# A projection slot between the value product and the score pair, and half-row groups 19 slots apart

## The chip, the core and the metric

The kernel runs on one core of a Trainium2 chip. Its engines work side by side, each through its own list of instructions: PE multiplies matrices (its weight loads are shown as PEld), DVE and ACT work element by element and both read PE's results out of PSUM, POOL masks, and SP issues the DMA transfers. The metric is the device time of one execution in microseconds (us); the time of a kernel is the median of its runs.

## The reference

One layer mixes sliding-window attention and a gated linear unit, weighted per token by a gate. There are 2048 tokens of 512 features, 32 heads of 16 features, a window of 256 tokens, and 1376 hidden features. All of it is float32.

```
x = A_x
g = sigmoid((x * gate_w).sum(-1, keepdims=True))
q, k, v = heads of x @ wqkv
scores = q k^T * 16 ** -0.5, masked to 0 <= i - j < 256
a = (softmax(scores) @ v) @ wo
b = (sigmoid(x @ w_gate) * (x @ w_up)) @ w_down
return g * a + (1 - g) * b
```

## The kernel before

**Precision.** A float32 operand is split into a rounded high part and a remainder, and a product is the sum of three matmuls (high by high, high by low, low by high). Features come in four blocks of 128 (`ND`), so one result tile of 128 by 512 takes 12 matmuls: such a set of 12 is called a group here.

**Stages.** The attention runs over `u` from 0 to 139 (`N`), in units of a group of four heads and a block of 128 tokens; there are 128 such units (`NU`). At `u`, `s_part(u, hh)` computes the scores of one head with queries on the partitions, and DVE takes their row maximum (`junk`, L307). `st_part(u - 9, hh)` computes the scores of an earlier unit transposed, with the maximum built into the operands, and ACT turns them into exponentials (`pt`, L352). POOL masks them. At every second `u`, ahead of the first head, `pv_part` multiplies the exponentials of the two units at `u - 12` and `u - 11` with V (L380): four heads side by side, each in a strip of 32 result columns, summed up in one bank `pv`. ACT then copies out half of `pv` (`o_take`, L396), and DVE clears it.

`s` and `st` of one iteration are a pair: each contracts over 64 rows, one in the upper and one in the lower half of the array, so that they run together. This is called a score pair.

**Slots.** Between the score pairs PE works off 111 groups: the projections of later heads (`pj`) and the gate and up products (`gu`). Each is cut into an upper and a lower half of its 128 contracted rows. The generator `turns()` counts slots `t`. In slot `t` it issues the upper-half matmul number `t`, and the lower-half matmul number `t - SHIFT`, which belongs to an earlier group; the two run together. A group's upper halves thus take slots 12i to 12i + 11 and its lower halves slots 12i + 18 to 12i + 29. A group holds one of three PSUM banks called `misc` from its first slot until ACT has copied it out. The generator yields after every third slot (`GAP`). The loop calls it once per head, not after the last head of an odd `u`: seven chunks of three slots in two `u`. From `u` = 128 on there are no more `s`, and it is called twice after every second head.

**Order.** The order on PE, ACT, DVE and SP is the order in which the program issues; the scheduler does not change it. Three lists put work off: `acts` (for ACT) and `behind` (for DVE) give up one entry at each head, and `later` holds stores, which SP issues at the start of the next `u`. When a group has its last slot, `turns()` puts its `post` (the copy out of PSUM) and its `after` (the next weights' rounding, where there is one) at the head of `acts`. They are issued in the next iteration, behind that one's score pair and exponential.

**The end.** A gate or up result goes out to scratch memory, and a last stage loads it again, multiplies with `w_down` (`pd`) and adds the attention part (`pa`). Three groups (`HOLD`) are kept back, with all 128 rows at once, to fill PE around the last value product.

Of the kernel before, what the change touches and what calls it, by code (L numbers as in the profile page):

```python
# [36 lines left out]
PVLAG = LAG + 2  # L37
# [1 line left out]
QB = 32  # L39
HOLD = 3  # L40
GAP = 3
SHIFT = 18
WD_LATE = {1: 8, 2: 9, 5: 10}
AHEAD = 5

# [2 lines left out]
def gated_mix_kernel(  # L48
# [48 lines left out]
    NU = NG * NB  # L97
# [20 lines left out]
    with ExitStack() as actx:  # L118
# [142 lines left out]
        def stack_build(t):  # L261
            sh, sl = (v.bitcast(F32) for v in stg.pop(t))
            rt = ring[t % RING].bitcast(F32)
            st = rt.rearrange("(a r) j f -> r a j f", r=4)
            dmas = [fill_rows(t % RING, 0, 0)]
            for low in range(2):
                for j in range(4):
                    for r in range(3):
                        if low == (r == (1 if j < 2 else 2)):
                            dmas.append((st[r + 1, :, j], (sl if low else sh)[32 * j:32 * j + 32]))  # L270
            return dmas

        def run_dmas(dmas):
            for dst, src in dmas:
                nc.sync.dma_start(dst, src)
# [92 lines left out]
        acts = []  # L368
        obs = {}

        def pv_part(u):
            g, j = divmod(u, NB)
            p = pts.pop(u)
            last = min(NB, j + 3)
            q = j
            while q < last:
                e = min(last, (q // 4 + 1) * 4)
                for hh in range(HG):
                    h = g * HG + hh
                    mm(  # L380
                        pv[32 * hh:32 * hh + 32, (q % 4) * P:(q % 4 + e - q) * P],
                        V[:, j, h * VW:h * VW + 32],
                        p[:, hh, (q - j) * P:(e - j) * P],
                        start=False, stop=True, skip_group_check=True,
                        tile_position=(0, 32 * hh),
                    )
                q = e
            if j % 2 == 1:
                acts.insert(0, lambda: o_take(g * NC + j // 4, j // 2 % 2))

        def o_take(s, half):
            g, c = divmod(s, NC)
            if half == 0:
                obs[s] = cpool.tile([P, CH], F32, tag="ob", name=f"ob{s}", bufs=2)
            cols = slice(2 * P * half, 2 * P * half + 2 * P)
            nc.scalar.copy(obs[s][:, cols], pv[:, cols])  # L396
            behind.insert(0, lambda: nc.vector.memset(pv[:, cols], 0.0))
            if half == 0:
                return
            ob = obs.pop(s)  # L400
            for hh in range(HG):
                h = g * HG + hh
                later.append((oT_d[h * DH:(h + 1) * DH, c * CH:(c + 1) * CH], ob[32 * hh:32 * hh + DH]))
            later.append((sum_d[c, g * HG:(g + 1) * HG], ob.rearrange("(h r) f -> r h f", r=32)[DH]))
# [38 lines left out]
        def load_gu(f, w):  # L443
            raw_gu[f, w] = cpool.tile([P, D], F32, tag="draw", name=f"guraw{f}_{w}", bufs=2)
            src = wgu[f, w] if FCH[f] == P else wgu_tail[w, :, :, 0:width(f, w)]
            nc.sync.dma_start(gu_half(raw_gu[f, w], width(f, w)), src)
# [72 lines left out]
        def turns():  # L519
            k3 = 3 * ND  # L520
            groups = []
            for t in range(n_rest * k3 + SHIFT):
                if t and t % GAP == 0:
                    yield
                if t % k3 == 0 and len(groups) < n_rest:
                    groups.append((work or rest).pop(0))
                for half, v in enumerate((t, t - SHIFT)):
                    if 0 <= v < n_rest * k3:
                        groups[v // k3][0](v % k3, half)
                if t >= SHIFT and (t - SHIFT) % k3 == k3 - 1:  # L530
                    _, after, post = groups[(t - SHIFT) // k3]
                    acts.insert(0, lambda after=after, post=post: (post(), after()))

        def flush(acts):
            while acts:
# [25 lines left out]
        def flat(v, c):  # L561
            return v[c].rearrange("h (q t) -> (h q) t", t=P)
# [5 lines left out]
        def sums_invert(c):  # L568
            t = sm.pop(c)
            nc.vector.reciprocal(t, t)  # L570
            return flat(rec_d, c), t

        def hold_group(step, _, post):
            for k in range(3 * ND):
                step(k)
            post()
# [7 lines left out]
        WD = NU - 5  # L584
        done = 0
        slots = turns()
        sdma = []

        for u in range(N):
            if u == LAG:  # L590
                vctx.close()
                ppool = actx.enter_context(tc.tile_pool(name="ppool", bufs=1))
            if u == 4:
                load_gu(0, 0)
                load_gu(0, 1)
            if u % 8 == 1 and u > 8 and u // 8 + 1 < NP:
                sdma = stack_build(u // 8 + 1)
            if u % 16 == 8 and u // 16 + 2 < NG:
                raw_q = load_wqk(u // 16 + 2)
            if u % 4 == 0 and 0 < u <= NU:  # L600
                max_store(u // 4 - 1)
            run_dmas(later)
            later.clear()
            run_dmas(sdma[:SD])
            del sdma[:SD]
            if u % 4 == 1 and 1 < u <= NU + 1:
                max_load(u // 4 - 1)
            if WD <= u < WD + 16 and (u - WD) % 2 == 0:
                load_d((u - WD) // 2)
            s4 = {1: 4, 5: 5, 9: 6, U_LAST: NSTEP - 2, U_LAST + 1: NSTEP - 1}.get(u)  # L610
            if u % 4 == 3 and u > LAG and (u + 2) // 4 + 4 < NSTEP - 2:
                s4 = (u + 2) // 4 + 4
            if s4 is not None:
                if u < LAG:
                    (work if u == 1 else first).append((3 * ND, lambda k, s4=s4: proj_mm(s4, k), lambda s4=s4: proj_post(s4)))
                else:
                    work.append(proj_group(s4))
            if u == NU + PVLAG - 1:
                hold_group(*rest.pop(0))
            for hh in range(HG):  # L620
                if hh == 0 and u % 2 == 0:
                    for w in (u - PVLAG - 1, u - PVLAG):
                        if 0 <= w < NU:
                            pv_part(w)
                if u < NU:
                    s_part(u, hh)
                if 0 <= u - LAG < NU:
                    st_part(u - LAG, hh ^ 1 if u < NU else hh)
                if u < LAG:
                    flush(behind)  # L630
                else:
                    if behind:
                        behind.pop(0)()
                    if acts:
                        acts.pop(0)()
                if u >= LAG and (hh < HG - 1 or u % 2 == 0 if u < NU else hh % 2 == 1):
                    next(slots, None)
                    if u >= NU:
                        next(slots, None)
            if u < LAG - 1:  # L640
                done += run_first(n_first * (u + 1) // LAG - done)
            elif u < LAG:
                run_first(n_first - done - 3 * ND)
                split_gu(0, 0)
                split_gu(0, 1)
                flush(acts)
                flush(behind)
                run_first(3 * ND)
                done = 0
            if u % 4 == 3 and u < NU:  # L650
                max_split(u // 4)
            if u // 16 + 2 < NG:
                if u % 16 == 13:
                    acts.append(lambda g=u // 16 + 2, r=raw_q: (
                        split_wqk(g, r, 0), behind.append(lambda: split_wqk(g, r, 1))))
            if 0 <= u - LAG < NU:
                mask_p(u - LAG)
            if WD + 2 <= u < WD + 10 and (u - WD) % 2 == 0:
                acts.append(lambda f=(u - WD) // 2 - 1: split_d(f, True))
            if SUMS <= u and (u - SUMS) % 4 == 0:  # L660
                sums_load((u - SUMS) // 4)
            if SUMS + 2 <= u and (u - SUMS) % 4 == 2:
                behind.append(lambda c=(u - SUMS) // 4: later.append(sums_invert(c)))
            if u >= HLOAD and (u - HLOAD) % 2 == 0:
                h_load((u - HLOAD) // 2)
            if u >= N - 2:
                flush(acts)
                flush(behind)
                h_skew(u - N - 1)
# [160 lines left out]
```

## Time and profile before

| | us |
|---|---|
| median of 3 runs | 756.0 |
| lowest and highest run | 755.45, 757.91 |
| the profiled execution | 755.79 |
| its span, first to last instruction | 754.1 |
| PE busy in the span | 745.9 |
| DVE busy | 483.7 |
| ACT busy | 436.2 |
| POOL busy | 171.9 |

In the lines of the profile, L233 is line 233 of the kernel. In the order in time, the columns are the start in us, the duration in us, the engine, the line, the operation, result and operands, the rows and columns of the array that a matmul or a weight load uses (64*128 is half the rows), and shapes; square brackets give the engine's idle time before it and what ended that. "x4" marks a run of equal instructions told as one. A matmul's start is recorded and its end is modelled. A weight load stands as PEld, ahead of its matmul. In the row by stage, the columns are the stretch and its length, then busy time and number of instructions of PE, PEld, DVE, ACT and POOL, PE's granted clock, and the DMA engines' busy share and rate. In a row that groups instructions, "mean ns" is the duration of one.

### The profile page before, as it was taken

The page shows a single profiled execution, that of the slowest core. Times are in us where ns is not written, and L with a number is a line of the kernel's source. Part 1 is how long each engine was busy: PE and PEld are TensorE (multiplying, and loading weights), DVE is VectorE, ACT ScalarE, POOL GpSimd, SP SyncE. Part 2 cuts the span into 40 slices and gives each one's busy share as a digit, 9 for nine tenths or more (in the row PEclk, how much of TensorE's full clock was granted, in tenths as well). Part 3 has the DMA queues.
Part 4 walks back from the last instruction along what each step waited for, and adds up shares of the span by engine and source line. Part 5 has one row for each costly group of instructions (what it writes and reads, how often), then busy time and mean ns, then how long its engine had stood idle before and what let it go on. Part 6 is the DMA issues. An engine that isn't in the chain of part 4 may idle for free.

```text
span 754.1 us, 17424 instructions
## 1 busy us (share of the span) xinstructions
PE 745.9 (99%) x6180; PEld 582.1 (77%) x6180; DVE 483.7 (64%) x1459; ACT 436.2 (58%) x930; POOL 171.9 (23%) x256
## 2 busy tenths in 40 slices
PE   8999999999999999999999999999999999999997
PEld 6877777787777877788787877778776778888886
DVE  5356767776776766776677676677522885749381
ACT  5412666666676667666666666656665562616241
POOL 7000233233233233323323322332321000000000
PEclk9999999999999999999999999999999999999999
DMA  8340434426444453444543525433455967557351
GB/s 305 95 113 19 108 100 120 124 76 172 120 105 125 118 143 111 115 112 123 139 126 85 149 68 162 141 108 118 128 179 157 270 214 224 178 190 226 122 154 56
DMA packets 69959, 103.58 MB, mean 137 GB/s; under 512 B 19314, under 2 KB 29042, under 8 KB 69872
## 3 DMA queue, kind: packets, MB, share of 16 engines
q1 hardware_dynamic: 69872, 102.48, 46.5%
q8 instruction: 48, 0.79, 0.4%
q14 instruction: 39, 0.32, 0.2%
HBM read 45.26 MB, written 32.00 MB: 102 GB/s over the span
## 4 chain that ended last, share of the span: by engine, by line
PE 95%; DMA 2%; DVE 1%; SPq 1%; issue 0%; ACT 0%; DVEq 0%; ACTq 0%
PE gu L233 34%; PE pj L233 12%; PE pv L380 11%; PE s L301 8%; PE st L347 5%; PE pd L70 4%; PE pd L72 4%; PE pd L71 4%; PE vps L70 2%; PE vps L72 2%; PE vps L71 2%; PE pa L70 2%; PE pa L72 2%; PE pa L71 2%; DMA woraw<-in_wo_dram 1%; DMA V<-in_xT_dram 1%
## 5 line engine op out<-in xcount | busy, mean ns | idle before, releaser
L307 DVE CUSTOM_DVE_ANT_0 junk<-s,mask 128x384 f32<-128x384 f32 (+2 forms) x512 | 272.1, 531 | 142.4 <-PE s L301 80.2
L233 PE MATMUL gu<-xh,w 64*128 64x512 f32 (+2 forms) x1384 | 344.4, 392 | 0.0
L352 ACT ACTIVATE pt<-st 128x384 f32<-128x384 f32 (+2 forms) x512 | 242.1, 474 | 170.4 <-PE st L347 69.9
L233 PE MATMUL gu<-xl,w 64*128 64x512 f32 (+3 forms) x692 | 227.4, 392 | 0.0
L233 PEld LDWEIGHTS gu<-xh,w 64*128 64x128 f32 (+2 forms) x1384 | 190.1, 183 | 19.5 <-issue 0.4
L357 POOL TENSOR_SCALAR_AFFINE_SELECT pt<-pt 128x512 f32<-128x512 f32 x128 | 88.1, 689 | 384.3 <-ACT pt L352 384.3
L347 PE MATMUL st<-ring 64*128 64x384 f32 (+2 forms) x536 | 169.7, 332 | 0.0
L301 PE MATMUL s<-ring 64*128 64x384 f32 (+2 forms) x536 | 165.7, 332 | 0.0
L301 PEld LDWEIGHTS s<-ring 64*128 64x128 f32 x536 | 94.4, 184 | 39.0 <-DVE nm L317 12.5
L233 PEld LDWEIGHTS gu<-xl,w 64*128 64x128 f32 (+3 forms) x692 | 107.9, 183 | 5.4
L347 PEld LDWEIGHTS st<-ring 64*128 64x128 f32 x536 | 97.1, 184 | 12.1 <-issue 2.7
L233 PE MATMUL pj<-xh,wqh 64*128 64x512 f32 (+1 forms) x232 | 91.5, 399 | 1.1 <-ACT xh L66 1.1
L380 PE MATMUL pv<-pt,V 128*32 128x384 f32 (+2 forms) x1408 | 91.0, 388 | 0.0
L233 PE MATMUL pj<-xl,wqh 64*128 64x512 f32 (+1 forms) x232 | 90.9, 397 | 0.0
L362 POOL TENSOR_SCALAR_AFFINE_SELECT pt<-pt 128x512 f32<-128x512 f32 x112 | 74.2, 663 | 0.0
L233 PE MATMUL pj<-xh,wql 64*128 64x512 f32 (+1 forms) x232 | 70.9, 392 | 0.0
L70 PE MATMUL pd<-ring,hb 128*128 128x512 f32 (+1 forms) x176 | 69.7, 396 | 1.1 <-ACT hb L66 1.1
L72 PE MATMUL pd<-ring,hb 128*128 128x512 f32 (+1 forms) x176 | 69.2, 393 | 0.5 <-DVE hb L67 0.4
L71 PE MATMUL pd<-ring,hb 128*128 128x512 f32 (+1 forms) x176 | 68.6, 390 | 0.4 <-DVE ring L111 0.4
L380 PEld LDWEIGHTS pv<-pt,V 128*32 128x32 f32 x1408 | 37.2, 109 | 36.0 <-issue 29.7
L66 ACT CAST hb<-V 128x512 fp32r<-128x512 f32 (+1 forms) x44 | 27.3, 620 | 55.0 <-DVE V L557 54.6
L471 ACT COPY sp<-gu 128x512 f32<-128x512 f32 (+2 forms) x88 | 51.1, 581 | 2.0 <-PE gu L233 2.0
(74 smaller groups left out, 903.5 us busy)
## 6 DMA issues: line engine op xcount, KB each, us to landing
gu_scratch<-sp SPq DMA_DIRECT2D x80, 256.0 KB
V<-gu_scratch SPq DMA_DIRECT2D x80, 256.0 KB
ring<-sh SPq DMA_DIRECT2D x128, 128.0 KB
ring<-sl SPq DMA_DIRECT2D x64, 128.0 KB
guraw<-in_wgu_dram SPq DMA_DIRECT2D x20, 256.0 KB
V<-in_xT_dram SPq DMA_DIRECT2D x16, 256.0 KB
oT_scratch<-ob SPq DMA_DIRECT2D x128, 32.0 KB
xl<-oT_scratch SPq DMA_DIRECT2D x16, 256.0 KB
```

The costliest lines, as they stand in the source:

```text
L70: mm(ps, lh, rh, start=first, stop=False)
L71: mm(ps, lh, rl, start=False, stop=False)
L72: mm(ps, ll, rh, start=False, stop=last)
L233: mm(pt[0:fw], (wl if w == 2 else wh)[r, d], (xl if w == 1 else xh)[r, d, c * CH:(c + 1) * CH], start=k == 0 and half != 1, stop=k == 3 * ...
L301: mm(pt[:, (k - k0) * P:(e - k0) * P], lhsT, blk(g, k, hh, 1, e - k), start=k == k0, stop=e == i + 1, skip_group_check=True,)
L307: nc.vector.tensor_tensor_reduce(junk[:, 0:n], pt[:, 0:n], mask[:, 3 * P - n:], scale=1.0, scalar=NEG, op0=ALU.add, op1=ALU.max, accum_out ...
L347: mm(pt[:, (q - j) * P:(e - j) * P], lhsT, blk(g, q, hh, 0, e - q), start=q == j, stop=e == last, skip_group_check=True,)
L352: nc.scalar.activation(pts[u][:, hh, 0:n], pt[:, 0:n], AF.Exp, scale=SCALE)
L357: nc.gpsimd.affine_select(p[:, :, 0:P], p[:, :, 0:P], pattern=[[0, HG], [1, P]], compare_op=ALU.is_ge, fill=0.0, base=0, channel_multiplie ...
L362: nc.gpsimd.affine_select(p[:, :, 2 * P:], p[:, :, 2 * P:], pattern=[[0, HG], [-1, P]], compare_op=ALU.is_gt, fill=0.0, base=0, channel_mu ...
L380: mm(pv[32 * hh:32 * hh + 32, (q % 4) * P:(q % 4 + e - q) * P], V[:, j, h * VW:h * VW + 32], p[:, hh, (q - j) * P:(e - j) * P], start=Fals ...
L471: nc.scalar.copy(t[0:width(f, w)], gp.pop((f, c, w))[0:width(f, w)])
```

## The change

`SHIFT` goes from 18 to 19. `turns()` yields after each slot, and the loop takes three at a time with `run_slots` (six in the tail). At an even `u` above 11 one slot, called the head slot, is issued between the value product and the score pair, and the same iteration's end (in the tail, that of the second head) has one slot fewer. `post` and `after` are issued at once, right behind the group's last slot, in place of being put at the head of `acts`.

```diff
-SHIFT = 18
+SHIFT = 19
...
             for t in range(n_rest * k3 + SHIFT):
-                if t and t % GAP == 0:
-                    yield
                 if t % k3 == 0 and len(groups) < n_rest:
                     groups.append((work or rest).pop(0))
                 for half, v in enumerate((t, t - SHIFT)):
...
                 if t >= SHIFT and (t - SHIFT) % k3 == k3 - 1:
                     _, after, post = groups[(t - SHIFT) // k3]
-                    acts.insert(0, lambda after=after, post=post: (post(), after()))
+                    post()
+                    after()
+                yield
...
+        def run_slots(n):
+            for _ in range(n):
+                next(slots, None)
...
                     for w in (u - PVLAG - 1, u - PVLAG):
                         if 0 <= w < NU:
                             pv_part(w)
+                head = u > PVLAG and hh == 0 and u % 2 == 0
+                if head:
+                    run_slots(1)
                 if u < NU:
                     s_part(u, hh)
...
                 if u >= LAG and (hh < HG - 1 or u % 2 == 0 if u < NU else hh % 2 == 1):
-                    next(slots, None)
-                    if u >= NU:
-                        next(slots, None)
+                    run_slots((GAP if u < NU else 2 * GAP) - (u > PVLAG and u % 2 == 0 and hh == (0 if u < NU else 1)))
```

## The prediction

> **What bounds the kernel now.** I read the page first, then the busy time by stage, then the order in time on the matrix engine around one value product. The page says that one engine fills the span.
>
> ```profile
> span 754.1 us, 17424 instructions
> PE 745.9 (99%) x6180; PEld 582.1 (77%) x6180; DVE 483.7 (64%) x1459; ACT 436.2 (58%) x930; POOL 171.9 (23%) x256
> ```
>
> The chain that ended last agrees:
>
> ```profile
> PE 95%; DMA 2%; DVE 1%; SPq 1%; issue 0%; ACT 0%; DVEq 0%; ACTq 0%
> ```
>
> The change acts from about 85 us (the first value product) to about 575 us (the last). The busy time by stage covers most of this in one row:
>
> ```profile
> 84.00:537.00 453.00, 453.00 (x4709) 353.31 (x4710) 320.64 (x1129) 300.03 (x678) 143.09 (x218) 1.00 0.43 120
> ```
>
> PE is busy for 453.00 of 453.00 us at granted clock 1.00, DVE for 71% and ACT for 66%. Ends of matmuls are modelled, so a busy PE can still hide holes; I therefore go by starts. In the undisturbed part of an iteration:
>
> ```profile
> 301.31 0.39 PE L233 MATMUL pj<-xl,wqh 64*128 64x512 f32 x1
> 301.54 0.39 PE L233 MATMUL pj<-xh,wqh 64*128 64x512 f32 x1
> 301.77 0.33 PE L301 MATMUL s<-ring 64*128 64x384 f32 x1
> 301.94 0.39 PE L233 MATMUL pj<-xl,wqh 64*128 64x512 f32 x1
> ```
>
> A projection slot (two half-row matmuls that start together; one of each pair is quoted) takes 0.23 us from start to start. A score pair (`s` and `st`) takes 0.17. Nothing waits here. Around a value product it is different:
>
> ```profile
> 302.64 0.33 PE L301 MATMUL s<-ring 64*128 64x384 f32 x1
> 302.90 0.53 PE L380 MATMUL pv<-pt,V 128*32 128x384 f32 x4
> ...
> 303.89 0.51 PE L380 MATMUL pv<-pt,V 128*32 128x384 f32 x4
> 304.33 0.44 PE L301 MATMUL s<-ring 64*128 64x384 f32 x1
> 304.33 0.44 PE L347 MATMUL st<-ring 64*128 64x384 f32 x1
> 304.61 0.38 PE L233 MATMUL pj<-xh,wqh 64*128 64x512 f32 x1
> ...
> 304.84 0.39 PE L233 MATMUL pj<-xl,wqh 64*128 64x512 f32 x1
> ```
>
> The score pair ahead of it holds PE for 0.26 instead of 0.17. The last four value matmuls start at 303.89 and the next work at 304.33, 0.44 later. The score pair behind them takes 0.28 instead of 0.17, so 0.11 more. The weight loads tell why:
>
> ```profile
> 303.25 0.13 PEld L380 LDWEIGHTS pv<-pt,V 128*32 128x32 f32 x4 [0.19 <-issue]
> 303.57 0.13 PEld L380 LDWEIGHTS pv<-pt,V 128*32 128x32 f32 x4 [0.19 <-issue]
> 304.33 0.18 PEld L301 LDWEIGHTS s<-ring 64*128 64x128 f32 x1 [0.62 <-DVE nm L317]
> 304.44 0.19 PEld L233 LDWEIGHTS pj<-xh,wqh 64*128 64x128 f32 x1
> ```
>
> One round of four value matmuls takes 0.32 (303.25 to 303.57), so 0.12 of the 0.44 is a hole after the last one. The load of `s` then starts with nothing left to cover it, and the next load follows at 304.44: 0.11 of bare load. The row names DVE's `nm` (L317) as the releaser, and this is the decisive reading. If the score pair really waited there, a slot ahead of it would fill the hole. If the hole belongs to the passage out of the value product, the slot falls into the same hole.
>
> **The change, part by part.**
>
> *One slot ahead of the score pair.* 63 value products (every second u from 12 to 136; 58 of them below u=128, the other five with `st` alone behind them) get a slot of two half-row matmuls behind them, and the iteration issues one slot fewer at its end. No matmul is added or removed by this part. The value product is still entered from a score pair and left once, so the 0.09 at entry (0.26 less 0.17) and the 0.12 hole stay. Before, exit reads: hole 0.12, bare load 0.11, pair 0.17, slot 0.23. After: hole 0.12, bare load 0.11, slot 0.23, pair 0.17. Same sum, 0.
>
> This needs the premise that a projection load, too, starts only behind the hole. The trace has one place where projection work follows a value product, with no score pair between: the last one, where a held-back full-row group comes behind.
>
> ```profile
> 575.79 0.29 PE L380 MATMUL pv<-pt,V 128*32 128x128 f32 x4
> 576.02 0.47 PE L233 MATMUL gu<-xh,w 128*96 128x512 f32 x1
> 576.33 0.39 PE L233 MATMUL gu<-xl,w 128*96 128x512 f32 x1
> 576.55 0.40 PE L233 MATMUL gu<-xh,w 128*96 128x512 f32 x1
> 576.02 0.16 PEld L233 LDWEIGHTS gu<-xh,w 128*96 128x96 f32 x1 [0.20 <-issue]
> 576.10 0.16 PEld L233 LDWEIGHTS gu<-xl,w 128*96 128x96 f32 x1
> ```
>
> Here 128 columns stream, a third of 384, so 0.11 of the 0.23 between 575.79 and 576.02, and 0.12 is the hole again. This load waited for nothing ("issue"), and it still came behind the hole; it is bare for 0.08 (576.02 to 576.10) with 96 weight columns against 0.11 with 128, and the first matmul holds PE for 0.31 instead of 0.22. So `s` isn't late because of DVE, and a slot put there pays the same. Bounds from this row: the bare load is 0.08 to 0.11, so the part is worth at most 0.03 a time, 63 x 0.03 = 1.9 us of gain, and as much of loss if a slot hides it worse; I take 0, since a half-row load has 128 columns like that of `s`.
>
> *Lower halves 19 slots behind.* 111 groups of 12 make 1332 + 18 = 1350 slots before and 1351 after. One slot, half empty, is added: +0.23 us on PE. The new distance also leaves five slots instead of six between the end of a group and the first matmul of the third next, which takes the same of the three `misc` banks.
>
> *The copy right behind the last slot.* A finished group used to be copied in the following iteration behind its exponential; now it is issued behind its last slot, which is the first of an iteration's three (or the head slot).
>
> ```profile
> 298.93 0.39 PE L233 MATMUL pj<-xh,wql 64*128 64x512 f32 x1
> 299.15 0.33 PE L347 MATMUL st<-ring 64*128 64x384 f32 x1
> 299.56 0.49 ACT L352 ACTIVATE pt<-st 128x384 f32<-128x384 f32 x1 [0.38 <-PE s L301]
> 299.94 0.58 ACT L245 COPY pr<-pj 128x512 f32<-128x512 f32 x1
> 300.49 0.49 ACT L352 ACTIVATE pt<-st 128x384 f32<-128x384 f32 x1
> 301.07 0.39 PE L233 MATMUL pj<-xh,wqh 64*128 64x512 f32 x1
> ```
>
> The group ends with the matmul of 298.93; the copy starts at 299.94, ends at 300.52, and the bank's next user starts at 301.07: 0.55 to spare, 0.32 ahead of its weight load one slot earlier. After the change the last slot comes one score pair and one slot later, at 298.93 + 0.23 + 0.17 = 299.33. An exponential starts 0.41 after its pair (299.15 to 299.56); for 512 columns I add the 0.06 by which a slot is longer than a pair, 299.33 + 0.47 = 299.80. ACT is still in the exponential until 299.94. The copy stays where it was, and so does the margin: 0.
>
> The exception is a group whose last slot is the head slot. Seven chunks of three slots make two u's and four chunks a group, so this is every seventh group, 15 of 111. Before, they were copied in the iteration without slots, while the value product ran:
>
> ```profile
> 85.53 0.58 ACT L245 COPY pr<-pj 128x512 f32<-128x512 f32 x1
> 87.04 0.49 ACT L352 ACTIVATE pt<-st 128x384 f32<-128x384 f32 x1 [0.93 <-PE st L347]
> 87.42 0.37 ACT L396 COPY ob<-pv 128x256 f32<-128x256 f32 x1
> 87.85 0.49 ACT L352 ACTIVATE pt<-st 128x384 f32<-128x384 f32 x1
> ```
>
> That cover (0.93 idle on ACT) goes. Now the copy stands ahead of the first exponential, and behind it queue that exponential, the copy of the value sums and the second exponential. Set 0 at the first load behind the value product. The head slot's data is ready at 0.11 + 0.47 = 0.58; the copy occupies ACT for 0.55 (299.94 to 300.49), until 1.13; the exponential ends at 1.62. The third score pair needs its bank. It is due at 1.84 before and after, with its load at 1.61:
>
> ```profile
> 305.94 0.18 PEld L301 LDWEIGHTS s<-ring 64*128 64x128 f32 x1
> 306.17 0.34 PE L301 MATMUL s<-ring 64*128 64x384 f32 x1
> ```
>
> So its load is 0.01 late, and 0.05 of slack is there (a load takes 0.18, the slot ahead 0.23). Without the copy the exponential would start at 0.34 + 0.41 = 0.75 and end at 1.24; the copy makes it 0.38 later. The cost is between 0 and that 0.38 each, 0 to 5.7 us; I take 0.02 each, 0.3 us, since the sum comes out at the edge. In the other iterations the exponential and DVE's maximum merely come 0.23 later:
>
> ```profile
> 304.81 0.56 DVE L307 CUSTOM_DVE_ANT_0 junk<-s,mask 128x384 f32<-128x384 f32 x1 [0.21 <-PE st L347]
> ```
>
> The maximum ends at 305.37, the third `s` starts at 306.17: 0.80 to spare becomes 0.57. Covered.
>
> *Queues.* Copies of the 15 groups reach SP's list one u later, so their stores to scratch go out about 4 us later, and `guraw` loads likewise; nothing reads those stores before the last u's. The pieces of `ring` that share SP's list keep their u. The cost is 0; without that cover a late `ring` piece would stall PE for up to those 4 us, for each of the three or so projection groups (23 of 111) among the 15.
>
> **Sum.** The profiled execution took 755.79 us, 754.1 in the span and 1.7 around it; it lies 0.2 under the median of 756.0. To it come 0 + 0.23 + 0.3 = 0.5: 756.3 us.
>
> **The rivals.** *A, the load slips under the value product (faster).* The slot waits for no DVE or ACT, so the sequencer could load its weights while the value product streams; the bare load goes, 63 x 0.11 = 6.9 us, 749.4; with half of it 752.9. For it: the DVE releaser in the `s` row. Against it: the load at 576.02, which waited for nothing and came late. The Trainium skill, TensorE: Matmul & The Clock Gate, lists in the table at its head an engine queue that pulls weight loads ahead of matmuls in flight; by that A would hold. The trace agrees between slots and score pairs (the load at 304.44 runs under `s`), and not behind a value product. There the skill's TensorEngine Tiling (Array Packing), section Key Properties, fits: a change of tiling mode drains the engine, and the value product works in strips of 32 columns.
>
> *B, ACT becomes the wait at the head (slower).* At the 15 groups the copy pushes back two exponentials and the value copy. It decides once the exponential ends later than 1.66 on the clock above; then the third pair, and for groups with a rounding pass behind them the next u's first pair, is late by what the copy adds. At the full 0.38 each this is 5.7 us in place of 0.3: 761.7; at half, 758.9. For it: the margin computed is nothing. Against it: an iteration without a value product (0.86, from 3 x 0.23 + 0.17) asks ACT for one exponential that holds it for 0.38 (299.56 to 299.94), so a lateness is made up in the next iteration.
>
> *C, the change does not do what it says*, because the compiler or the slot iterator puts the matmuls in the old order: 756.0. Against it: the order on PE, ACT, DVE and SP is written out by hand in this kernel, and the loop issues the slot between the two. I give it no chance of its own; its time is within that of the forecast.
>
> **How the numbers follow.** Runs of this kernel differ by 0.3% (755.45 to 757.91), so anything within 0.3%, 2.3 us, I call no change. Forecast 0.64, A in whole or part 0.20, B in whole or half 0.16. The likeliest's own range is 754.4 (the 1.9 of gain) to 758.2 (the 1.9 of loss). With half of A below and half of B above the range is 752.0 to 759.2. Faster by over 0.3%: 0.20, all of A. Slower: 0.16, B. Within: 0.64.
>
> **What would show it.** In the new profile the load behind the value product should be that of a projection slot, starting 0.44 after the start of the last four value matmuls (of 384 columns), the score pair 0.34 after it and the next slot 0.17 behind that. If the load starts while value matmuls stream, or the pair comes 0.23 behind, A is right. If the third score pair's load after a head shows a wait for an exponential, B is. PE busy short of the full stage, or a `ring` piece named as a releaser, would prove the forecast wrong in a way that I haven't priced.

## The result and the profile after

| | before | after |
|---|---|---|
| median of 13 runs, us | 756.46 | 759.13 |
| lowest and highest, us | 755.45, 758.21 | 757.32, 760.75 |
| the profiled execution, us | 755.79 | 758.46 |
| its span, us | 754.1 | 756.7 |

The ratio is 1.0033, with a 95% interval of 1.0022 to 1.0043: the change costs about 2.5 us. The 759.13 lies inside the predicted range, 0.07 below its upper end. The forecast called anything within 0.3% no change; 0.33% is just over that, and the interval reaches to both sides of it. The forecast expected 0.5 us more than before, and the place of the loss was not the one it had priced.

The spans alone don't say where the 2.6 us went, because both ends of the kernel vary from run to run (last section). The two rows per kernel below, of the views by tile, give the first and the last start of the value matmuls and of the last stage's matmuls (the figures with slashes are shortest, median and longest duration in ns). Before:

```profile
L380 PE MATMUL pv<-pt,V x1408: 272/379/511, 85.0 to 575.8; 128*32 128x384 f32 x64, 128*32 128x256 f32 x56, 128*32 128x128 f32 x56
L70 PE MATMUL pd<-ring,hb x176: 392/394/501, 581.6 to 738.5; 128*128 128x512 f32 x160, 96*128 96x512 f32 x16
```

After:

```profile
L380 PE MATMUL pv<-pt,V x1408: 272/379/511, 85.7 to 578.9; 128*32 128x384 f32 x64, 128*32 128x256 f32 x56, 128*32 128x128 f32 x56
L70 PE MATMUL pd<-ring,hb x176: 388/394/505, 584.7 to 741.1; 128*128 128x512 f32 x160, 96*128 96x512 f32 x16
```

From the first value matmul to the first matmul of the last stage it is 581.6 - 85.0 = 496.6 us before and 584.7 - 85.7 = 499.0 after: 2.4 longer. I call this the stretch; with two decimals it is 496.59 and 499.00. It holds nearly all that the change touches. The half-row slots begin a little earlier, but from the first of them to the first value matmul it is 9.06 us before (75.97 to 85.03) and 9.05 after (76.62 to 85.67). The stretch repeats far better than a run: in the last experiment below, u = 12 to 127 take as long as before to 0.00 us.

**The passage out of the value product is as predicted.** The first rows are PE, the last two its weight loads, of the changed kernel:

```profile
305.48 0.51 PE L380 MATMUL pv<-pt,V 128*32 128x384 f32 x4
305.92 0.50 PE L233 MATMUL pj<-xh,wqh 64*128 64x512 f32 x1
306.26 0.33 PE L301 MATMUL s<-ring 64*128 64x384 f32 x1
306.43 0.39 PE L233 MATMUL pj<-xl,wqh 64*128 64x512 f32 x1
305.92 0.18 PEld L233 LDWEIGHTS pj<-xh,wqh 64*128 64x128 f32 x1 [0.62 <-issue]
306.02 0.19 PEld L301 LDWEIGHTS s<-ring 64*128 64x128 f32 x1
```

The slot starts 0.44 behind the start of the last four value matmuls, as the score pair did before; the pair follows 0.34 later and the next slot 0.17 behind that. The bare load stays, 0.10 here (305.92 to 306.02). The releaser is now "issue": no engine kept the slot waiting, and it came no sooner than the score pair had. The DVE instruction that the row of before named as the releaser of `s` had not held it up. The Trainium skill, TensorEngine Tiling (Array Packing), section Key Properties, says that a change of tiling mode drains the engine; this trace agrees, with a hole of 0.12 (the 0.44 less 0.32 for a round of four) ahead of the slot as ahead of the score pair.

**The loss has places.** Going by the start of each value product, nearly every two u's take as long as before, to 0.03 us. The exceptions are u = 14, 30, 46, 62, 78, 94 and 126, by 0.21 to 0.23 each, 1.5 in all, and the tail from u = 128 on, by 0.81. The first of them, in rows before and after (start of the value products of u = 14 and 16):

```profile
92.93 0.64 PE L380 MATMUL pv<-pt,V 128*32 128x256 f32 x8
100.82 0.85 PE L380 MATMUL pv<-pt,V 128*32 128x384 f32 x8
```

```profile
93.56 0.42 PE L380 MATMUL pv<-pt,V 128*32 128x256 f32 x4
101.68 0.53 PE L380 MATMUL pv<-pt,V 128*32 128x384 f32 x4
```

That is 7.89 before and 8.12 after. Inside these two u's, ACT of the kernel before:

```profile
95.74 0.49 ACT L352 ACTIVATE pt<-st 128x384 f32<-128x384 f32 x1
96.13 0.58 ACT L245 COPY pr<-pj 128x512 f32<-128x512 f32 x1
96.60 0.51 ACT L352 ACTIVATE pt<-st 128x384 f32<-128x384 f32 x1
96.99 0.62 ACT L142 CAST wqh<-wqraw 128x512 fp32r<-128x512 f32 x1
```

And of the changed kernel ACT, then PE, then the weight load:

```profile
96.44 0.51 ACT L352 ACTIVATE pt<-st 128x384 f32<-128x384 f32 x1
96.83 0.63 ACT L142 CAST wqh<-wqraw 128x512 fp32r<-128x512 f32 x1
97.33 0.61 ACT L245 COPY pr<-pj 128x512 f32<-128x512 f32 x1
97.81 0.53 ACT L352 ACTIVATE pt<-st 128x384 f32<-128x384 f32 x1
...
97.72 0.33 PE L347 MATMUL st<-ring 64*128 64x384 f32 x1
98.00 0.49 PE L233 MATMUL gu<-xh,w 64*128 64x512 f32 x1
98.34 0.62 PE L233 MATMUL gu<-xh,w 64*128 64x512 f32 x2
...
98.00 0.18 PEld L233 LDWEIGHTS gu<-xh,w 64*128 64x128 f32 x1 [0.32 <-ACT pr L245]
```

The reader should see the two ACT lists trade places. Before, the copy of the finished group (L245) stood right behind an exponential, and the rounding of the next projection weights (L142) came an iteration later. After, the rounding stands ahead of the copy and holds ACT for 0.50 (96.83 to 97.33). The copy ends at 97.94. The next user of its bank was due one pair behind 97.72, at 97.89; its weight load waits for the copy and starts at 98.00. The lateness is 0.11, but the loss here is twice that: the load itself had no matmul to run under, so the slot holds PE for 0.34 (98.00 to 98.34) instead of 0.23. The view of waits of the changed kernel has this wait six times, once for each of u = 14 to 94 in the list above:

```profile
PEld gu L233 <- ACT pr L245: 1.9, 6, 0.3
```

These rows give who waited for whom, the total in us, the times and the longest. At u = 126 the copy is that of a gate or up result (L471), and the rounding ahead of it another one (L110). The view of the kernel before has no wait of a slot's load for either copy.

### The profile page after: what moved, and what is told of

It reads as the page before. It is cut to its first block, busy times and chain, and to the rows that moved or that the text cites. A ratio compares the mean times of both kernels' runs of the same rounds, so it can differ in the third digit from the quotient of the medians.

```text
span 756.7 us, 17519 instructions
## 1 busy us (share of the span) xinstructions
PE 748.4 (99%) x6180; PEld 575.8 (76%) x6180; DVE 480.4 (63%) x1459; ACT 431.9 (57%) x930; POOL 165.8 (22%) x256
## 4 chain that ended last, share of the span: by engine, by line
PE 95%; DMA 3%; DVE 1%; ACT 1%; issue 0%; SPq 0%; DVEq 0%; ACTq 0%
PE gu L233 36%; PE pj L233 12%; PE pv L380 11%; PE st L347 6%; PE s L301 6%; PE pd L70 4%; PE pd L72 4%; PE pd L71 4%; PE vps L70 2%; DMA V<-gu_scratch 2%; PE vps L71 2%; PE vps L72 2%; PE pa L72 2%; PE pa L70 2%; PE pa L71 2%; DMA wdraw<-in_wd_dram 1%
## 5 line engine op out<-in xcount | busy, mean ns | idle before, releaser
L307 DVE CUSTOM_DVE_ANT_0 junk<-s,mask 128x384 f32<-128x384 f32 (+2 forms) x512 | 272.0, 531 | 146.8 <-PE st L347 66.4
L233 PE MATMUL gu<-xh,w 64*128 64x512 f32 (+3 forms) x1384 | 359.5, 397 | 0.0
L233 PE MATMUL gu<-xl,w 64*128 64x512 f32 (+3 forms) x692 | 245.9, 397 | 0.0
L233 PEld LDWEIGHTS gu<-xh,w 64*128 64x128 f32 (+3 forms) x1384 | 204.5, 183 | 34.8 <-issue 10.5
L357 POOL TENSOR_SCALAR_AFFINE_SELECT pt<-pt 128x512 f32<-128x512 f32 x128 | 85.3, 666 | 392.1 <-ACT pt L352 392.1
L347 PE MATMUL st<-ring 64*128 64x384 f32 (+2 forms) x536 | 163.3, 317 | 0.0
L301 PE MATMUL s<-ring 64*128 64x384 f32 (+2 forms) x536 | 159.5, 320 | 0.0
L233 PEld LDWEIGHTS gu<-xl,w 64*128 64x128 f32 (+3 forms) x692 | 124.2, 183 | 13.2 <-issue 6.4
L233 PE MATMUL pj<-xh,wqh 64*128 64x512 f32 (+1 forms) x232 | 95.4, 414 | 1.3 <-ACT xh L66 1.3
L233 PE MATMUL pj<-xh,wql 64*128 64x512 f32 (+1 forms) x232 | 74.2, 398 | 0.0
L362 POOL TENSOR_SCALAR_AFFINE_SELECT pt<-pt 128x512 f32<-128x512 f32 x112 | 70.9, 633 | 0.0
L471 ACT COPY sp<-gu 128x512 f32<-128x512 f32 (+2 forms) x88 | 51.4, 585 | 21.1 <-PE gu L233 19.7
```

What stands on the lines that cost most here:

```text
L233: mm(pt[0:fw], (wl if w == 2 else wh)[r, d], (xl if w == 1 else xh)[r, d, c * CH:(c + 1) * CH], start=k == 0 and half != 1, stop=k == 3 * ...
L301: mm(pt[:, (k - k0) * P:(e - k0) * P], lhsT, blk(g, k, hh, 1, e - k), start=k == k0, stop=e == i + 1, skip_group_check=True,)
L307: nc.vector.tensor_tensor_reduce(junk[:, 0:n], pt[:, 0:n], mask[:, 3 * P - n:], scale=1.0, scalar=NEG, op0=ALU.add, op1=ALU.max, accum_out ...
L347: mm(pt[:, (q - j) * P:(e - j) * P], lhsT, blk(g, q, hh, 0, e - q), start=q == j, stop=e == last, skip_group_check=True,)
L357: nc.gpsimd.affine_select(p[:, :, 0:P], p[:, :, 0:P], pattern=[[0, HG], [1, P]], compare_op=ALU.is_ge, fill=0.0, base=0, channel_multiplie ...
L362: nc.gpsimd.affine_select(p[:, :, 2 * P:], p[:, :, 2 * P:], pattern=[[0, HG], [-1, P]], compare_op=ALU.is_gt, fill=0.0, base=0, channel_mu ...
```

## The experiments

The table gives the stretch of the profiled execution and the ratio of the runs to those of the kernel before, with its interval. Runs scatter by some 3 us, so the stretch and the places in it carry the verdicts.

| | stretch, us | u = 12 to 127, against before | u from 128, against before | ratio of runs (95%) |
|---|---|---|---|---|
| changed kernel | 499.00 | +1.61 | +0.81 | 1.0033 (1.0022 to 1.0043) |
| head slot alone | 497.43 | +0.07 | +0.77 | 1.0006 (0.9993 to 1.0020) |
| list entry behind the slots | 497.74 | +0.65 | +0.51 | 1.0024 (1.0009 to 1.0039) |
| distance 18 | 497.68 | +0.41 | +0.69 | 1.0017 (1.0004 to 1.0030) |
| distance 19 alone | 544.27 | +35.27 | +12.41 | 1.0635 (1.0611 to 1.0659) |
| rounding one u earlier | 498.82 | +1.43 | +0.81 | 1.0054 (1.0032 to 1.0077) |
| no head slot in the tail | 498.14 | +1.61 | -0.05 | 1.0032 (1.0019 to 1.0045) |
| rounding ahead of the copy, in the old kernel | 497.56 | +1.01 | -0.03 | 1.0014 (1.0001 to 1.0027) |
| distance 18, no head slot in the tail | 496.80 | +0.42 | -0.20 | 0.9997 (0.9982 to 1.0012) |
| rounding one u later | 497.80 | +0.32 | +0.90 | 1.0021 (1.0004 to 1.0038) |
| copy behind the last slot, alone | 496.43 | 0.00 | -0.16 | 1.0006 (0.9991 to 1.0022) |

**The three parts apart.** The head slot alone, in the kernel with distance 18 and the copy through ACT's list:

```diff
-SHIFT = 19
+SHIFT = 18
...
-                    post()
-                    after()
+                    acts.insert(0, lambda after=after, post=post: (post(), after()))
```

> The kernel before with the head slot alone: distance 18, and a finished group copied in the following iteration, ahead of whatever else waits for ACT there. Theory T (the time is lost where another rounding of ACT stands ahead of the copy of a finished group, so that the third next group waits for its bank): no such place here, 0.0 us against before, at most 0.5 either way. Rival R1 (the head slot itself costs, in the passage out of the value product): all of the loss, +2.4 us. Rival R2 (the distance of 19 costs by itself, a slot more and one slot less to spare at each of 111 groups): 0.0.

Below u = 128 it costs 0.07 us over 58 value products, so R1 is out there. In the tail it costs 0.77: 0.23 to 0.24 at each of u = 128, 130 and 132 and 0.10 at 134. With that the whole is 0.85, more than the 0.5 that T allowed for. The rows are ACT's around u = 130, first of the kernel before, then of this one, each with PE's two `st` pairs behind them (both matmuls of a pair stand in one row):

```profile
546.59 0.49 ACT L352 ACTIVATE pt<-st 128x384 f32<-128x384 f32 x1 [2.04 <-PE st L347]
547.23 0.51 ACT L352 ACTIVATE pt<-st 128x384 f32<-128x384 f32 x1
...
546.05 0.44 PE L347 MATMUL st<-ring 64*128 64x384 f32 x2
547.69 0.54 PE L347 MATMUL st<-ring 64*128 64x384 f32 x2
```

```profile
547.11 0.49 ACT L352 ACTIVATE pt<-st 128x384 f32<-128x384 f32 x1 [2.26 <-PE st L347]
547.75 0.51 ACT L352 ACTIVATE pt<-st 128x384 f32<-128x384 f32 x1
...
546.66 0.37 PE L347 MATMUL st<-ring 64*128 64x384 f32 x2
547.97 0.78 PE L347 MATMUL st<-ring 64*128 64x384 f32 x2
548.31 0.18 PEld L347 LDWEIGHTS st<-ring 64*128 64x128 f32 x1 [0.38 <-ACT pt L352]
```

In the tail both heads of a pair give ACT an exponential at once, and the next pair needs both their banks. Before, the second exponential ends at 547.23 + 0.51 = 547.74, and the second pair's matmuls run from 547.69 to 548.23; with the head slot it ends at 548.26, a weight load of the pair starts at 548.31, and the matmuls end at 548.75. Both ends are 0.52 later; 0.29 of that is there from the start, since this value product began at 544.91 instead of 544.62, and 0.23 is new. The second pair was already waiting for ACT, and a slot put ahead of the first pair delays the exponentials by its whole length.

The list entry behind the slots, so that the copy is always first:

```diff
-                    if acts:
-                        acts.pop(0)()
...
                     run_slots((GAP if u < NU else 2 * GAP) - (u > PVLAG and u % 2 == 0 and hh == (0 if u < NU else 1)))
+                if u >= LAG and acts:
+                    acts.pop(0)()
```

> The changed kernel, with one line moved: the list of ACT's put-off work gives up its entry behind the iteration's slots in place of ahead of them, so the copy of a finished group always comes first. T: the seven losses of 0.21 us at u = 14, 30, 46, 62, 78, 94, 126 and most of the 0.4 at u = 132 go, 1.9 of 2.4; it stands at +0.2 to +0.6 us against before, and the wait of a projection's weight load for ACT's copy is gone from the trace. R1 and R2: +2.4 us, as the changed kernel.

The losses of 0.21 shrink to 0.06 and less, the one of 0.43 at u = 132 to 0.07, and no load waits for either copy any more. 1.3 of the 2.4 went where 1.9 were expected: small delays of up to 0.06 are now spread over the u's below 128. In the view of waits the score pair's load now waits for DVE's maximum (L307) 13 times in place of 2, which would fit, but no run tests it. The interval of the runs is too wide to tell this kernel from the changed one.

The distance back at 18, with head slot and copy kept (`SHIFT = 18`, one line):

> The changed kernel with the distance back at 18: head slot and copy behind the last slot stay. The last slot is now the third of an iteration, so the copy is issued ahead of the next exponential and has six slots. T: no wait for a bank, one slot fewer: 0.0 us against before, at most 0.4 either way. R1: +2.4. R2: 0.0.

The large losses go here too, and so does the 0.24 at the end of the tail, which is the added slot. What stays in the tail, 0.69, is the head slot's; below u = 128 another 0.41 stays in small delays, whose cause is open. The 1.1 in all is more than the 0.4 that T allowed. The distance of 19 alone, in the kernel before (`SHIFT = 19`, one line):

> The kernel before with the distance of 19 alone: the copy still goes through ACT's list, so it comes an iteration later (0.87 us) for a bank that had 0.55 us to spare, and 0.3 of these for the weight load. T: 0.3 to 0.5 us at each of the some 80 groups that have no value product between copy and next user, +25 to +40 us. R2 in its plain form (one slot and one slot's spare): +0.2 to +2.4.

47.7 us, above the 25 to 40 that T gave; 35.3 of it lies below u = 128 and 12.4 in the tail. The wait is where T puts it:

```profile
PEld gu L233 <- ACT sp L471: 35.0, 49, 2.0
PEld gu L233 <- ACT pr L245: 8.2, 14, 0.6
PEld pj L233 <- ACT pr L245: 7.2, 11, 0.7
```

So the copy behind the last slot isn't an extra: the distance of 19 can't be had without it.

**Which work stands ahead of the copy.** The rounding of projection weights one u earlier:

```diff
-                if u % 16 == 13:
+                if u % 16 == 12:
                     acts.append(lambda g=u // 16 + 2, r=raw_q: (
```

> The changed kernel; the rounding of the next projection weights is put on ACT's list one u earlier (behind u = 12, 28, ... in place of 13, 29, ...), nothing else. Measured by the trace, from the first value matmul to the first matmul of the last stage: 496.6 us before, 499.0 after. T: this rounding is what stands ahead of the copy at u = 14, 30, 46, 62, 78, 94; the six losses of 0.21 go, u = 126 (another rounding) keeps its own: 499.0 - 1.3 = 497.7. Rival R3 (the copy is late there because of the pattern of groups, whatever stands ahead): the losses stay or move, 499.0.

The losses did not go. They moved, from u = 14 to the two u's of 12, 28, 44, 60, 76 and 92, by 0.18 to 0.19 each. Rows of ACT and the weight load:

```profile
93.03 0.49 ACT L352 ACTIVATE pt<-st 128x384 f32<-128x384 f32 x1 [0.43 <-PE st L347]
93.42 0.61 ACT L142 CAST wqh<-wqraw 128x512 fp32r<-128x512 f32 x1
93.93 0.59 ACT L471 COPY sp<-gu 128x512 f32<-128x512 f32 x1
...
94.56 0.18 PEld L233 LDWEIGHTS gu<-xh,w 64*128 64x128 f32 x1 [0.30 <-ACT sp L471]
```

The rounding again stands ahead of a copy, that of the group before. My expectation had overlooked that a group ends at every fourth chunk of slots, and that a chunk at the first head of u = 13 is one of them. The loss travels with the rounding, which favours T, but it ends nowhere, which R3 allows. So the rounding was put one u later (`u % 16 == 14`), where its entry comes up at a head without a group's end:

> The changed kernel with the rounding of the next projection weights one u later (at u = 15, 31, ...). One u earlier it met the copy of another group, at the first head of u = 13. At the first head of u = 15 no group ends. T: the six losses go without a new place, 499.0 - 1.3 = 497.7 us from the first value matmul to the last stage. R3 (the pattern of groups, whatever stands ahead): a loss of 0.2 at u = 14 or 15 stays, 499.0.

All six losses are gone, and no new one has come; 1.2 of the stretch, as expected. R3 falls. ACT's rows show the two apart: the copy of the group at u = 14 directly behind its exponential, and the rounding in an iteration of its own.

```profile
97.44 0.51 ACT L352 ACTIVATE pt<-st 128x384 f32<-128x384 f32 x1
97.82 0.61 ACT L245 COPY pr<-pj 128x512 f32<-128x512 f32 x1
...
100.44 0.61 ACT L142 CAST wqh<-wqraw 128x512 fp32r<-128x512 f32 x1
100.95 0.49 ACT L352 ACTIVATE pt<-st 128x384 f32<-128x384 f32 x1
101.33 0.59 ACT L471 COPY sp<-gu 128x512 f32<-128x512 f32 x1
```

The other way round, the loss is put into the old kernel: distance 18, no head slot, only the order of the two pieces of work turned where both wait.

```diff
-                    acts.insert(0, lambda after=after, post=post: (post(), after()))
+                    acts.insert(0, lambda after=after, post=post: (acts and acts.pop(0)(), post(), after()))
```

> The kernel before, distance 18, no head slot; only where an entry of ACT's list waits when a finished group is copied, that entry goes ahead of the copy. The same stretch, 496.6 before. T: the losses appear in the old kernel at u = 14, 30, 46, 62, 78, 94 and 126, 0.2 each, 1.5 in all and up to 0.4 in the tail, 498.0 to 498.5. If the head slot or the distance of 19 is needed for them as well: 496.6 to 496.9.

Losses appear at u = 14, 30, 46, 62, 78, 94 and 126, the same seven and no others, by 0.14 to 0.15 each. That is 1.0 in place of the 1.5 expected, and the tail loses nothing. The order of the two is enough for the loss, without a head slot and at the old distance. The first of them:

```profile
98.74 0.33 PE L301 MATMUL s<-ring 64*128 64x384 f32 x1
98.95 0.50 PE L233 MATMUL gu<-xh,w 64*128 64x512 f32 x2
99.29 0.40 PE L233 MATMUL gu<-xl,w 64*128 64x512 f32 x2
98.95 0.19 PEld L233 LDWEIGHTS gu<-xh,w 64*128 64x128 f32 x2 [0.25 <-ACT pr L245]
```

The slot was due at 98.91 (98.74 and 0.17) and comes 0.04 late; then it holds PE for 0.34 (98.95 to 99.29) as in the changed kernel. So a place costs 0.15 here and 0.21 to 0.23 there because the wait is 0.04 in place of 0.11; the 0.11 of bare load is the same. Why the wait is shorter, no run shows.

**The tail.** The changed kernel with the head slot only below u = 128:

```diff
-                head = u > PVLAG and hh == 0 and u % 2 == 0
+                head = PVLAG < u < NU and hh == 0 and u % 2 == 0
...
-                    run_slots((GAP if u < NU else 2 * GAP) - (u > PVLAG and u % 2 == 0 and hh == (0 if u < NU else 1)))
+                    run_slots((GAP if u < NU else 2 * GAP) - head)
```

> The changed kernel with the head slot only below u = 128; in the tail all six slots follow the score pair again. The same stretch of the trace, 499.0 after. T2 (in the tail the second pair waits for the exponentials of the first, so the slot ahead of the first pair is paid in full, 0.2 for two u's): what u = 128 to 135 lost, 0.57, shrinks by 0.3 to 0.6, 498.4 to 498.7. Rival R4 (the tail loses by the later copy alone): 499.0.

The tail gains 0.86 where 0.3 to 0.6 were expected, so R4 falls and T2 holds, at a larger size. What is left there has two signs. u = 128, 130 and 134 now stand 0.16 to 0.21 under the kernel before; in the changed kernel this gain hid most of the head slot's cost, and they stood 0.00 to 0.09 over it. u = 132 stays 0.24 over it, where a slot's load waits 0.29 for a copy (L471), as at u = 126, and u = 136 stays 0.26 over, the added slot. The medians of runs do not follow (1.0032): 0.9 us is less than they resolve. With the distance of 18 as well:

> The changed kernel with distance 18 and the head slot only below u = 128: the head slot and the copy behind the last slot, without the added slot, the late copies and the tail. T and T2: nothing is left to lose, 496.6 to 497.0 in the stretch, the time of before within 0.5 us. R1 (the passage out of the value product): 498.5 or more.

496.80, and the runs say 0.9997: head slot and copy behind the last slot, without the rest, are the kernel before to 0.2 us. Last, the copy alone:

```diff
-                    acts.insert(0, lambda after=after, post=post: (post(), after()))
+                    post()
+                    after()
```

> The kernel before with the third part alone: distance 18, no head slot, a finished group copied right behind its last slot. The run without a head slot in the tail stood 0.2 under the kernel before in each two u's of the tail. If that is the copy's gain, this kernel stands 0.2 to 0.6 us under before in the stretch, 496.0 to 496.4, and beats both by less than runs can tell (ratio 0.999 to 1.000). If the head slot below u = 128 is part of it: 496.6.

The stretch is 0.16 shorter than before, 0.02%, all of it at u = 134, and just short of the 0.2 to 0.6 expected. That is the best stretch of all, and far too little for runs to show (1.0006, 0.9991 to 1.0022). None of these kernels beats the kernel before by a margin that can be measured.

## Why the prediction came out as it did

- *One slot ahead of the score pair: 0.* Right for the 58 value products below u = 128: the exit rows follow the predicted 0.44, 0.34 and 0.17, and the part alone costs 0.07 us there. Wrong for the five in the tail. Their `st` pairs were counted along with the rest, but in the tail the second pair waits for the first one's exponentials, and the slot is paid in full at three of the five. Alone it costs 0.77 there.
- *A slot more: 0.23.* Right; the last two u's with slots lose 0.24 in the changed kernel, and nothing in the runs with distance 18.
- *The copy stays where it was, and so does the margin: 0.* This is the step that failed. It followed one copy, at 299.94, where ACT had nothing but exponentials around it. ACT's list also gives up one entry at each head, between the exponential and the slots. Putting the copy at the head of that list had let it pass all entries; issuing it behind the slots lets the entry that comes up pass the copy. The weights' rounding of 0.50 then eats the margin, which the prediction had put at 0.55 and at 0.32 ahead of the load. Seven places at 0.21 to 0.23 make 1.5 us, the larger part of the 2.4.
- *15 copies at head slots, 0.3 in all (rival B).* The queue was drawn rightly and the cost is nothing. The first of them, at u = 12 of the changed kernel:

```profile
87.64 0.59 ACT L245 COPY pr<-pj 128x512 f32<-128x512 f32 x1 [1.38 <-PE pj L233]
88.12 0.50 ACT L352 ACTIVATE pt<-st 128x384 f32<-128x384 f32 x1
88.51 0.38 ACT L396 COPY ob<-pv 128x256 f32<-128x256 f32 x1
...
87.10 0.50 PE L233 MATMUL pj<-xh,wqh 64*128 64x512 f32 x1
88.95 0.33 PE L301 MATMUL s<-ring 64*128 64x384 f32 x1
```

  The copy starts 0.54 behind the first load (0.58 was worked out), the exponential ends at 1.52 (1.62), and the third pair comes at 1.85 (1.84): on time. These two u's take 7.90 before and after. The 14 others, at every eighth u up to 124, lose no more than 0.03 either. B's mechanism, PE waiting for ACT behind a head slot, was real after all, but in the tail, where the prediction did not look for it.
- *Rival A, a load under the value product.* It did not happen; the load of 305.92 waited for nothing and came behind the hole.
- *The size.* In the stretch 0.23 + 1.5 + 0.57 for the rest of the tail make 2.3 of the 2.4, against 0.5 predicted. The measured time is in the range that half of B had opened, but for the most part by a step that B doesn't contain. That it falls inside is luck: the working gives 758.9 for half of B, the stated end of 759.2 is 0.3 above that without a reason given, and 759.13 lies in this margin. The range of the likeliest case alone, up to 758.2, missed it.
- *A count.* The 23 projection groups among the 111 are 26 (the kernel before copies one out 26 times at L245). Of the 15 copies at head slots one is a projection's, and not three or so. Nothing in the sum hangs on either.

## What to carry to other kernels

When a step is moved in an engine's hand-written order, list everything that can come up between its old and its new place, not only the work that is there in one sample of the trace. Fixed periods lock: here a group ends at every fourth chunk, 16 u's hold 56 chunks, and a piece of work that comes once in 16 u's meets a group's end either never or every time. And look at the tail by itself, since a stage with a different ratio of work per engine can be bound by what is hidden elsewhere.

## What was not expected of the hardware

A late weight load costs more than its wait. At 98.00 of the changed kernel the slot came 0.11 late, and the load, which otherwise runs under the previous matmuls, added 0.11 of its own. At 98.95 of the old kernel with the rounding ahead of the copy, the slot came only 0.04 late, and the load added the same 0.11.

The start of the kernel varies by 3 us between profiled executions, in a part that no edit touched: the first value matmul starts at 85.0 us in the kernel before and at 88.1 in the last experiment. The row by stage for 10 to 20 us shows part of it, before and then in that experiment; the three figures at the end of a row are PE's granted clock, the DMA engines' busy share and their rate.

```profile
10.00:20.00 10.00, 10.00 (x44) 8.14 (x45) 5.68 (x9) 5.95 (x11) 4.84 (x4) 1.00 0.90 333
```

```profile
10.00:20.00 10.00, 10.00 (x34) 7.79 (x34) 6.68 (x11) 6.29 (x12) 4.81 (x4) 0.76 0.97 339
```

PE did 34 matmuls in these 10 us instead of 44, at a granted clock of 0.76 instead of 1.00. In the later execution PE had waited more for its first inputs (6.16 us of work in the first 10, against 7.61). That the waits lowered the clock is likely, but no run was made to show it. For a change of 0.3% this scatter is as large as the effect, and only a stretch of the trace that leaves the start out can place it.
